# Gated layer of a two-part mix: all products stored first, then the down projection by 128-row blocks

## The chip, the core and the metric

The kernel runs on one core of a Trainium2 chip. The core has a matmul engine (TensorE, PE in the rows, with PEld for its weight loads), three engines for elementwise work (VectorE = DVE, ScalarE = ACT, GpSimd = POOL), and SyncE (SP), which here issues DMAs and passes on signals. The metric is the device time of one execution in microseconds; smaller is better.

## The reference

The input x has 2048 rows of 640 numbers, in four chunks of 512 rows. Two layers work on it and a gate per row mixes them:

```
x = A_x
g = _sigmoid((x * gate_w).sum(-1, keepdims=True))
a = _A_ref(x, A_wq, A_wk, A_wv, A_wo, A_beta)     # attention within a chunk, and a memory over chunks
b = _B_ref(x, B_w1, B_w3, B_w2)
return g * a + (1 - g) * b

def _B_ref(x, w1, w3, w2):                        # the gated layer
    gate = jnp.einsum("bsd,df->bsf", x, w1)
    up = jnp.einsum("bsd,df->bsf", x, w3)
    h = _silu(gate) * up                          # f = 1728
    return jnp.einsum("bsf,fd->bsd", h, w2)
```

Attention has 32 heads of 20 numbers. The change is about the gated layer alone.

## The kernel before

**Numbers.** Matmuls run in a reduced fp32 form (fp32r). For accuracy each operand is split into a high part (ScalarE casts it) and a low part (a subtraction on GpSimd or VectorE), and each product takes three passes (high by high, high by low, low by high; `PASSES`). `split` (line 172) does this to a weight.

**Halves of the array.** Nearly every product (a `Work`) is divided by its inner dimension: array rows 0 to 63 take one half of the 128, rows 64 to 127 the other, and both add to one PSUM bank. `halves` (line 254) makes the two lists. The two halves run at once on different works: while one work is in the second half, the next is in the first. Where a work moves from the first half to the second, an empty instruction on SyncE (`w.seen`, line 270) passes the signal. So SyncE's queue, which issues most DMAs, also stands in this path.

**Order.** The kernel writes every engine's order out itself. A planner keeps clocks of what each engine would do (`busy`, `clocks`, `heap`) and decides from them which instruction is written next; the program that results has a fixed order for each engine, with semaphores between them. A stream of dense works (projections and the gated layer) is pulled by `step`; attention comes in between by slots (`attention`, `S_AT`, `T_AT`): scores s with row maxima on VectorE, then transposed scores t, exponentials on ScalarE, a mask on GpSimd, and the weighted sums o. `segs` says which dense works lie beside which heads.

**Weights.** `w_add` puts a weight on a list. `w_load` brings item k into one of three raw buffers (`NRAW`); `w_split` splits it into one of eight tiles W (`NW`); `w_get` hands it to a matmul. Both are run in advance by `w_step`, or at once where a matmul needs the tile. `floors` and `set_oldest` say which tiles must still be kept. After a split the raw buffer counts as free only `FREE` = 2000 ns later.

**Gated layer.** w1 and w3 have 13 blocks of 128 columns and one (number 13, `NF`) of 64. For each pair of chunks, A = (0, 1) and B = (2, 3), and each block j, `ffn_up` makes g (gate) and u (up) for both chunks: ScalarE takes a tanh, VectorE multiplies twice, which leaves the product in a tile ft of 128 by 512. Then ScalarE copies it into ht (high) and GpSimd subtracts (low, line 1034). ht tiles are six (`NHT`). Because so few products fit, up and down alternate: five groups (`GROUPS`) of two or three blocks, and after each group `ffn_down` multiplies the ht tiles by the w2 blocks for every 128 rows (lb) and half of the 640 columns (hf), 8 tiles f per chunk. The first group's f is scaled and written to acc (ScalarE), the others are added to acc (VectorE, line 1103).

The attention's transfers qk<-qkd are issued by GpSimd (`load_pair`), between its splits. The attention's output projection is op (`oproj`); its adds to acc and those of f end the program, with the last stores.

Of the kernel before, what the change touches and what calls it, by code (L numbers as in the profile page):

```python
# [20 lines left out]
P = 128  # L21
# [9 lines left out]
NST, NW, NRAW, NHT, NVG, NB, FREE = 4, 8, 3, 6, 2, 8, 2000  # L31
# [9 lines left out]
R1H, R1B = 19, 3  # L41
COL, COL4, MIN_MM, APART, ISSUE, AHEAD = 0.4533, 1.7, 62, 5, 580, 1500
# [3 lines left out]
LAND, SPARE, NOP = 4200, 99999, 80  # L46
# [4 lines left out]
def gated_mix(ctx: ExitStack, tc: tile.TileContext, xT, wqk, wv, w13, w2, w2h, wo, beta, out):  # L51
# [9 lines left out]
    od = [dp.tile([H, 32, L], F32, name=f"od{c}") for c in range(NSEG)]  # L61
    gd = [dp.tile([P, 4, D], F32, name=f"gd{c}") for c in range(NSEG)]
# [109 lines left out]
    def split(dst, src, lo=None, ns=600, done=None, bank=None):  # L172

        def low():

            def sub(e):
                return lambda: e.tensor_sub(dst[:, 1], src, dst[:, 0].bitcast(F32))  # L177

            dve, pool = ("dve", 1.4 * ns, sub(nc.vector)), ("pool", 2.15 * ns, sub(nc.gpsimd))
            return dve if lo or busy["dve"] + dve[1] + SPARE < max(busy["pool"], now()) + pool[1] else pool  # L180

        stages(bank, ("act", ns, lambda: nc.scalar.copy(dst[:, 0], src)), low, done=done)  # L182
# [287 lines left out]
    def w_add(src, n, queue=nc.sync):  # L470
        items.append((src, n, queue))
        return len(items) - 1
# [6 lines left out]
    def limit():  # L479
        return NW + clock["oldest"] - sum(h < clock["oldest"] for s in floors.values() for h in s)  # L480
# [4 lines left out]
    def w_load():  # L485
        k = clock["next"]
        src, n, queue = items[k]
# [12 lines left out]
    def w_split():  # L500
        k, raw, n, _ = raws.pop(0)
        assert k < limit()
        w = sp.tile([P, 2, D + 2], FR, tag="W", name=f"W{k}", bufs=NW)
        halfway.add(k)

        def done():
            tiles[k] = w
            halfway.remove(k)
            if k not in EARLY:
                freed.append(now() + FREE)  # L510

        split(w[:, :, :n], raw[:, :n], k < NW, 730, done)

    halfway = set()

    def w_step():
# [8 lines left out]
        if clock["next"] < min(len(items), limit() + NRAW) and \  # L525
# [3 lines left out]
    def w_get(i):  # L529

        while i not in tiles:
# [5 lines left out]
            elif i in halfway:  # L537
                force()
# [88 lines left out]
    def new_x(c):  # L627
# [4 lines left out]
        while ("x", c - 2) in floors:  # L632
# [356 lines left out]
    def plan_down(js):  # L989
        return [w_add(w2[j] if j < NF else w2h, D) for j in js]  # L990

    hts = {}

    def ffn_up(cs, j, idx, oldest=None, by_weight=False, free=None, last=None):
        half = j == NF
        fs = {}

        def evac_gate(c):

            def evac(pg, bank):  # L1000
# [8 lines left out]
                a, b = (slice(0, 64), slice(64, P))[::-1 if c not in TURNED else 1]  # L1009
                u = f_tile(f"fu{c}_{j}")  # L1010
                ht = ht_tile([P, 2, L], FR, f"ht{c}_{j}")

                def end():
                    let(f"ft{c}_{j}")
                    let(f"fu{c}_{j}")
                    hts[c, j] = ht

                stages(bank, ("act", 600, lambda: nc.scalar.activation(t[:64], pg[:64], AF.Tanh, scale=0.5)),
                       ("dve", 690, lambda: nc.vector.scalar_tensor_tensor(u[64:], t[:64], 1.0, pg[:64], op0=ALU.add, op1=ALU.mult)),
                       ("dve", 690, lambda: nc.vector.scalar_tensor_tensor(pg[a], u[64:], 0.5, pg[64:], op0=ALU.mult, op1=ALU.mult)),  # L1020
                       ("act", 600, lambda: nc.scalar.copy(ht[a, 0], pg[a])),
                       ("dve", 690, lambda: nc.vector.tensor_sub(ht[b, 0], pg[a], ht[a, 0].bitcast(F32)), True), done=end)
            return evac

        def evac_up(c):

            def evac(pu, bank):
                ht = ht_tile([P, 2, L], FR, f"ht{c}_{j}")
# [3 lines left out]

                def low():
                    nc.gpsimd.tensor_sub(ht[:, 1], t, ht[:, 0].bitcast(F32))  # L1034

                def end():
                    let(f"ft{c}_{j}")
                    hts[c, j] = ht

                stages(bank, ("dve", 690, lambda: nc.vector.scalar_tensor_tensor(t, t, 0.5, pu, op0=ALU.mult, op1=ALU.mult), True),  # L1040
                       ("act", 620, lambda: nc.scalar.copy(ht[:, 0], t)), ("pool", 1290, low), done=end)  # L1041
# [3 lines left out]
        if by_weight:  # L1045
            todo.sort(key=lambda e: e[1])
        for n, (c, k) in enumerate(todo):
            old = min(idx[e[1]] for e in todo[n:]) if oldest is None else oldest
            name, evac = (("g", evac_gate(c)), ("u", evac_up(c)))[k]

            def end(ps, bank, evac=evac, n=n, c=c, k=k):
                evac(ps, bank)
                if last is not None:
                    last(c, j, idx[k])
                if free in floors and n == len(todo) - 1:
                    del floors[free]
# [5 lines left out]
    def ffn_down(cs, js, idx, last=False, free=None):  # L1062
        first = js[0] == 0
        def tile_of(c, lb, hf):

            def parts(ps):
                todo = [(j, i, a, b) for j, i in zip(js, idx) for a, b in (PASSES if j < NF else ((0, 0), (0, 1)))]
                return halves([lambda j=j, i=i, a=a, b=b: (ps[:, :320], hts[c, j][:, a, lb * P:(lb + 1) * P],
                                                           w_get(i)[:, b, 320 * hf:320 * hf + 320], 320 * COL)
                               for j, i, a, b in todo], 0, (c in TURNED, 3 * js.index(NF) + 1) if NF in js else None)  # L1070
# [12 lines left out]
            def evac(ps, bank):  # L1083
# [22 lines left out]
                if (lb, hf) == (3, 1):  # L1106
                    for j in js:
                        let(f"ht{c}_{j}")
                if free in floors and (c, lb, hf) == (cs[-1], 3, 1):
                    del floors[free]  # L1110

            return Work(f"f{c}_{js[0]}_{lb}_{hf}", parts, evac, idx[0], None, lambda: all((c, j) in hts for j in js) and (
                not first or c < NSEG - 1 or all(("out", 1, q) in landed for q in range(4))))

        for c in cs:
            if first:
                accs[c] = slot(f"acc{c}")[:, :4 * D].rearrange("p (b d) -> p b d", b=4)
            for lb in range(4):
                for hf in range(2):
                    yield tile_of(c, lb, hf)  # L1120
# [412 lines left out]
    GROUPS = [[0, 1, 2], [3, 4, 5], [6, 7, 8], [9, 10, 11], [13, 12], [9, 10], [13, 11, 12]]  # L1533

    def job_up(cs, j, by_weight=False):
        return (4 if j < NF else 2) * 3.5, ffn_up(cs, j, plan_up([j])[0], by_weight=by_weight)

    def woven(cs, j, c, first, mid):

        plan, key = plan_up([j])[0], ("w", cs, j)  # L1540
        floors[key] = set(plan)
        u = ffn_up(cs, j, plan, free=key)
        o1, o2 = jobs_oproj(c)

        def mix():
            yield from islice(o2[1], 4)
            yield from islice(u, mid)
            yield from o2[1]
            yield from u

        return o1, (3.5 * first, islice(u, first)), (3.5 * (4 - first) + o2[0], mix())

    def down_with_out(cs, g, c, mid):

        plan = plan_wo()
        floors["o", c] = held = set(plan)
        o1, o2 = oproj(c, plan, held)
        cost, f = job_down(cs, g)

        def mix():  # L1560
            yield from islice(o2, 4)
            yield from islice(f, mid)
            yield from o2
            yield from f

# [226 lines left out]
```

## Time and profile before

| | |
|---|---|
| three timed runs | 1077.18, 1077.37, 1078.13 us; median 1077.37 |
| profiled execution, first to last instruction | 1077.5 us |
| busy: TensorE, VectorE, ScalarE, GpSimd | 1070.5, 574.7, 491.0, 569.8 us |
| weight loads of TensorE (they overlap matmuls) | 975.3 us |
| moved by DMA | 154.98 MB, 144 GB/s on average |
| granted TensorE clock, mean | 0.998 |

No time for the profiled execution beyond its span is given; the span lies among the timed runs. In a group's row stand line, engine, operation, output<-inputs, shapes and count, then busy time (overlaps counted once), the mean length of one in ns, and the idle time of the engine before them, with what ended it. In the chain of waits a row has start, length, and the instruction. In a window's row stand the stretch, its length, busy time (and count) of PE, PEld, DVE, ACT and POOL, granted clock, DMA share and GB/s.

### The profile page before, as it was taken

The page shows a single profiled execution, that of the slowest core. Times are in us where ns is not written, and L with a number is a line of the kernel's source. Part 1 is how long each engine was busy: PE and PEld are TensorE (multiplying, and loading weights), DVE is VectorE, ACT ScalarE, POOL GpSimd, SP SyncE. Part 2 cuts the span into 40 slices and gives each one's busy share as a digit, 9 for nine tenths or more (in the row PEclk, how much of TensorE's full clock was granted, in tenths as well). Part 3 has the DMA queues.
Part 4 walks back from the last instruction along what each step waited for, and adds up shares of the span by engine and source line. Part 5 has one row for each costly group of instructions (what it writes and reads, how often), then busy time and mean ns, then how long its engine had stood idle before and what let it go on. Part 6 is the DMA issues. An engine that isn't in the chain of part 4 may idle for free.

```text
span 1077.5 us, 29709 instructions
## 1 busy us (share of the span) xinstructions
PE 1070.5 (99%) x11681; PEld 975.3 (91%) x11681; DVE 574.7 (53%) x1742; ACT 491.0 (46%) x1013; POOL 569.8 (53%) x765
## 2 busy tenths in 40 slices
PE   9999999999999999999999999999999999999998
PEld 7999999988998989889989989999889889888998
DVE  6022575345555666666454566663446666553464
ACT  6255434544344343465655664446442443344221
POOL 3543446366466464556664555655663854564340
PEclk9999999999999999999999999999999999999999
DMA  9465753243344331637585886554434542442231
GB/s 320 133 213 188 260 159 103 76 117 99 82 122 115 100 90 51 185 97 254 169 251 182 248 294 193 159 158 131 132 92 110 149 111 78 113 118 67 61 99 74
DMA packets 88099, 154.98 MB, mean 144 GB/s; under 512 B 19628, under 2 KB 34904, under 8 KB 87960
## 3 DMA queue, kind: packets, MB, share of 16 engines
q1 hardware_dynamic: 56520, 96.88, 27.7%
q0 software_dynamic: 23664, 42.04, 15.8%
q10 hardware_dynamic: 7776, 14.16, 3.7%
q8 instruction: 93, 1.52, 0.6%
q14 instruction: 46, 0.38, 0.1%
HBM read 97.55 MB, written 54.53 MB: 141 GB/s over the span
## 4 chain that ended last, share of the span: by engine, by line
PE 97%; DMA 1%; POOL 1%; issue 0%; ACT 0%; DVE 0%; POOLq 0%
PE g L267 19%; PE u L267 17%; PE f L267 16%; PE k L267 7%; PE o L1253 7%; PE v L267 7%; PE op L267 7%; PE q L267 5%; PE s L1158 4%; PE t L1220 4%; PE q L779 1%; PE pm L267 1%; PE nd L267 1%; DMA qk<-qkd 1%; PE pkt L265 0%; PE gt L265 0%
## 5 line engine op out<-in xcount | busy, mean ns | idle before, releaser
L267 PE MATMUL g<-X,W 64*128 64x512 f32 x1680 | 397.8, 395 | 0.0
L267 PE MATMUL u<-X,W 64*128 64x512 f32 x1560 | 378.8, 395 | 0.0
L1169 DVE CUSTOM_DVE_ANT_0 junk<-s,mask 128x128 bf16<-128x128 f32 (+3 forms) x512 | 251.2, 491 | 174.1 <-PE s L1158 135.7
L267 PEld LDWEIGHTS g<-X,W 64*128 64x128 f32 x1680 | 276.2, 185 | 13.4 <-issue 2.4
L177 POOL TENSOR_TENSOR W<-wr,W 128x640 fp32r<-128x640 f32 (+1 forms) x132 | 206.2, 1570 | 151.7 <-ACT W L182 139.0
L267 PE MATMUL f<-W,ht 64*128 64x320 f32 x2592 | 278.5, 309 | 0.0
L267 PEld LDWEIGHTS u<-X,W 64*128 64x128 f32 x1560 | 262.2, 185 | 9.6 <-issue 0.6
L267 PEld LDWEIGHTS f<-W,ht 64*128 64x128 f32 x2592 | 262.2, 187 | 2.2 <-issue 1.4
L1227 ACT ACTIVATE P<-t 128x384 f32<-128x384 f32 (+1 forms) x384 | 181.1, 525 | 148.8 <-PE t L1220 129.4
L1236 POOL TENSOR_SCALAR_AFFINE_SELECT P<-P 128x256 f32<-128x256 f32 (+1 forms) x192 | 93.5, 496 | 194.9 <-ACT P L1227 180.0
L182 ACT CAST W<-wr 128x640 fp32r<-128x640 f32 (+1 forms) x138 | 97.4, 726 | 43.6 <-PE u L267 24.9
L267 PE MATMUL k<-X,W 64*128 64x512 f32 x600 | 107.9, 399 | 0.0
L267 PE MATMUL op<-W,oT 64*128 64x320 f32 x960 | 103.5, 307 | 0.0
L267 PEld LDWEIGHTS op<-W,oT 64*128 64x128 f32 x960 | 97.8, 185 | 1.2 <-issue 0.8
L1103 DVE SCALAR_TENSOR_TENSOR acc<-f,cgate,acc 128x320 f32<-128x320 f32 x126 | 67.8, 547 | 55.8 <-PE f L267 52.7
L1158 PE MATMUL s<-qk 60*128 60x256 f32 (+2 forms) x512 | 90.1, 326 | 2.1 <-DMA qk<-qkd 2.1
L267 PE MATMUL v<-W,X 64*128 64x320 f32 (+2 forms) x948 | 90.7, 310 | 0.0
L1220 PE MATMUL t<-qk 62*128 62x256 f32 (+2 forms) x512 | 89.6, 324 | 0.0
L1034 POOL TENSOR_TENSOR ht<-ft,ht 128x512 fp32r<-128x512 f32 x52 | 67.2, 1293 | 41.0 <-ACT ht L1041 40.7
L1179 POOL DMA_DIRECT2D qk<-mr x128 | 73.4, 574 | 27.6 <-DVE mr L1195 25.5
L267 PEld LDWEIGHTS v<-W,X 64*128 64x128 f32 (+1 forms) x948 | 86.7, 186 | 0.6 <-issue 0.2
L267 PEld LDWEIGHTS k<-X,W 64*128 64x128 f32 x600 | 82.2, 185 | 3.6 <-issue 0.2
(121 smaller groups left out, 1307.2 us busy)
## 6 DMA issues: line engine op xcount, KB each, us to landing
qk<-qkd POOLq DMA_DIRECT2D x128, 240.0 KB, 4.0
wr<-in_w_dram SPq DMA_DIRECT2D x80, 320.0 KB
qkd<-qs SPq DMA_DIRECT2D x20, 512.0 KB
qkd<-ks SPq DMA_DIRECT2D x20, 512.0 KB
od<-oq ACTq DMA_DIRECT2D x32, 256.0 KB
wr<-in_wo_dram SPq DMA_DIRECT2D x20, 320.0 KB
vg<-vd SPq DMA_DIRECT2D x16, 336.0 KB
qkd<-qs SPq DMA_DIRECT2D x20, 256.0 KB
```

Of the source, the lines that this page charges most:

```text
L177: return lambda: e.tensor_sub(dst[:, 1], src, dst[:, 0].bitcast(F32))
L182: stages(bank, ("act", ns, lambda: nc.scalar.copy(dst[:, 0], src)), low, done=done)
L267: ins = nc.tensor.matmul(o, l, x, start=i == 0 and (r == 0 or not w.todo[0]), stop=i == len(todo) - 1 and (r == 1 or not w.todo[1]), skip_ ...
L1034: nc.gpsimd.tensor_sub(ht[:, 1], t, ht[:, 0].bitcast(F32))
L1103: nc.vector.scalar_tensor_tensor(dst, ps[:, :320], cgate[:, c, lb:lb + 1], dst, op0=ALU.mult, op1=ALU.add)
L1158: nc.tensor.matmul(ps[i][:, o:o + n], q[:, qb * P:(qb + 1) * P], k[:, :n], start=qb != 1, stop=qb != 0, skip_group_check=True)
L1169: nc.vector.tensor_tensor_reduce(out=junk[:, :n], in0=ps[i][:, o:o + n], in1=mask[:, L - n:], scale=1.0, scalar=-3.0e38, op0=ALU.add, op1= ...
L1179: nc.gpsimd.dma_start(dst, src)
L1220: nc.tensor.matmul(ps[i][:, o:o + L - q0], k[:, kb * P:(kb + 1) * P], q[:, q0:], start=kb != 2, stop=kb != 3, skip_group_check=True)
L1227: nc.scalar.activation(u["P"][:, i, o:o + n], ps[i][:, b:b + n], AF.Exp, scale=SCALE)
L1236: nc.gpsimd.affine_select(d, d, pattern=[[0, 2], [0, n], [1, P]], base=0, channel_multiplier=-1, compare_op=ALU.is_ge, fill=0.0)
L1253: nc.tensor.matmul(ps[32 * i:32 * i + 32, kb * P:], heads[2 * p + i]["v"][:, kb], pairs[p + i // 2]["P"][:, i % 2, o:o + n], start=kb == 0 ...
```

## The change

Up and down no longer alternate. `ffn_up` runs for all 14 blocks of a pair of chunks. Its product ft is not split; it is stored to a new DRAM tensor `hd` (60 stores by SyncE, from `send`), laid out by blocks of 128 rows. Then `ffn_down` runs in three groups of 4, 5 and 5 blocks of w2. For each group, chunk and block of 128 rows one item of the weights' list is the product itself: 128 by 512 or 640 numbers, loaded from `hd` like a weight (48 loads) and split like one. The two column halves of f use it in turn. VectorE takes a split of these items or of w2 when the planner finds it sooner there (`EVEN`). In groups 1 and 2, four of the five w2 blocks lie in what was a chunk's X tile (`home`, tile XW), since X is not needed once the products are made.

Buffers: W tiles 8 to 9, raw buffers 3 to 4, ht tiles 6 to 4. A raw buffer of such an item counts as free 700 ns after its split (`SOON`), not 2000. The helpers for mixed up and down work (`woven`, `down_with_out`, `jobs_up_by_chunk` and others) go, and the lists of segments are written anew: the output projections now follow f tiles of whole groups.

```diff
-NST, NW, NRAW, NHT, NVG, NB, FREE = 4, 8, 3, 6, 2, 8, 2000
+NST, NW, NRAW, NHT, NVG, NB, FREE = 4, 9, 4, 4, 2, 8, 2000
...
+    hd = [dp.tile([4, 3, P, D], F32, name=f"hd{c}") for c in range(NSEG)]
...
     def w_split():
         k, raw, n, _ = raws.pop(0)
         assert k < limit()
-        w = sp.tile([P, 2, D + 2], FR, tag="W", name=f"W{k}", bufs=NW)
+        home = items[k][5]
+        if home is None:
+            w = sp.tile([P, 2, D + 2], FR, tag="W", name=f"W{k}", bufs=NW)
+        else:
+            c, i = home
+            if i == 0:
+                homes[c] = cp.tile([P, 2, KB, L], FR, tag="X", name=f"XW{c}", bufs=2)
+            w = homes[c].rearrange("p a k l -> p (a k l)").rearrange("p (i a n) -> p i a n", i=4, a=2)[:, i]
...
-                freed.append(now() + FREE)
+                freed.append(now() + (FREE if items[k][4] is False else SOON))
...
-        split(w[:, :, :n], raw[:, :n], k < NW, 730, done)
+        split(w[:, :, :n], raw[:, :n], k < 8, 730 * n / D, done, spare=EVEN if items[k][4] else SPARE)
...
+        def send(c, t):
+            name = f"ft{c}_{j}"
+            todo = [(slice(0, 64), t[64:]), (slice(64, P), t[64:])] if half else [(slice(0, P), t)]
...
+            for k, src in list(todo):
+                dst = hd[c][:, g, k, n * P:(n + 1) * P].rearrange("b p n -> p b n")
+                store_later(dst, src.rearrange("p (b n) -> p b n", n=P), ("h", c, j, k.start), done=end)
...
-                def low():
-                    nc.gpsimd.tensor_sub(ht[:, 1], t, ht[:, 0].bitcast(F32))
...
                 stages(bank, ("dve", 690, lambda: nc.vector.scalar_tensor_tensor(t, t, 0.5, pu, op0=ALU.mult, op1=ALU.mult), True),
-                       ("act", 620, lambda: nc.scalar.copy(ht[:, 0], t)), ("pool", 1290, low), done=end)
+                       done=lambda: send(c, t))
...
-    GROUPS = [[0, 1, 2], [3, 4, 5], [6, 7, 8], [9, 10, 11], [13, 12], [9, 10], [13, 11, 12]]
+    GROUPS = [[0, 1, 2, 3], [4, 5, 6, 7, 8], [9, 10, 11, 12, 13]]
...
+    def job_down(cs, g, at=range(8), last=False):
+        js = GROUPS[g]
+        wi, after = plans.setdefault((cs, g), []), plans.setdefault((cs, g + 1), [])
+        wi += [plan_down(cs, g, n) for n in range(len(wi), len(js))]
+        n = len(js) * P
+        hi = {}
+        for a in at:
+            c, lb = cs[a // 4], a % 4
+            hi[c, lb] = w_add(hd[c][lb, g, :, :n], n, even=True,
+                              needs=[("h", c, j, k) for j in js for k in ((0, 64) if j == NF else (0,))])
+            if a in NEXT[g]:
+                after.append(plan_down(cs, g + 1, len(after)))
...
-    tail = [braid(chain([d] + u + [d2, take(d3, 6)]), o1, 1400, 6000), alternate(take(o2, 7), take(d3, 0)), o2, d3]
+    d2 = job_down(B, 2, last=True)
+    o1, o2 = jobs_oproj(3)
+    tail = [braid(chain([d1b, take(d2, 14)]), o1, 1400, 6000), o2, d2]
```

What this does to the written order is shown at two places. The first is ScalarE where chunk 3 follows chunk 2 in the first down group of pair B. Before (acc_11654 is chunk 2's, acc_12115 chunk 3's; P are exponentials of t):

```order
L1087 ACTIVATE acc_11654<-f_0_1_1_11946,cgate 128x320
L1087 ACTIVATE acc_11654<-f_0_2_0_11973,cgate 128x320
L1087 ACTIVATE acc_11654<-f_0_2_1_12030,cgate 128x320
L1087 ACTIVATE acc_11654<-f_0_3_0_12053,cgate 128x320
L1227 ACTIVATE P_12058<-t_1_0_12166 128x384
L1227 ACTIVATE P_12058<-t_1_1_12167 128x384
L1087 ACTIVATE acc_11654<-f_0_3_1_12083,cgate 128x320
L182 CAST W_12202<-wr_12076 128x640
L1087 ACTIVATE acc_12115<-f_0_0_0_12117,cgate 128x320
L182 CAST W_12228<-wr_12109 128x640
```

ScalarE now, at the same place (acc_14629 is chunk 2's; W_14946 and W_14996 are the first two product blocks of chunk 3; oq is the copy of a group of weighted sums, od its store):

```order
L1110 ACTIVATE acc_14629<-f_0_1_0_14711,cgate 128x320
L184 CAST XW_14650<-wr_14761 128x640
L1110 ACTIVATE acc_14629<-f_0_1_1_14754,cgate 128x320
L1280 COPY oq_14936<-o_14919 128x512
L716 DMA od_79<-oq_14936 128x512
L184 CAST W_14946<-wr_14788 128x512
L1110 ACTIVATE acc_14629<-f_0_2_0_14790,cgate 128x320
L1249 ACTIVATE P_14956<-t_0_0_14957 128x512
L1249 ACTIVATE P_14956<-t_0_1_14958 128x512
L184 CAST XW_14650<-wr_14801 128x640
L1110 ACTIVATE acc_14629<-f_0_2_1_14826,cgate 128x320
L184 CAST W_14996<-wr_14845 128x512
```

The casts of product blocks and of the next group's w2 stand between the evacuations, and the cast of chunk 3's first block comes after the copy and the store of o.

VectorE takes the low parts of both blocks; its rows there now (L1191 are row maxima over scores s, two instructions each):

```order
L179 TENSOR_TENSOR XW_14650<-wr_14761,XW_14650 128x640
L179 TENSOR_TENSOR W_14946<-wr_14788,W_14946 128x512
L1191 ISA junk,m_14729<-s_1_0_14992,mask 128x384
L1191 ISA m_14729 128x1
L1191 ISA junk,m_14729<-s_1_1_14993,mask 128x384
L1191 ISA m_14729 128x1
L1191 ISA junk,m_14729<-s_2_0_15015,mask 128x512
L1191 ISA m_14729 128x1
L1191 ISA junk,m_14729<-s_2_1_15016,mask 128x512
L1191 ISA m_14729 128x1
L179 TENSOR_TENSOR W_14996<-wr_14845,W_14996 128x512
```

The second block's subtraction stands behind four row maxima.

The second place is the end of TensorE's queue. Before, its last rows are all in the second half of the array (op is the output projection of chunk 3, f its last down tiles):

```order
L267 MATMUL op_3_1_17407<-W_16714,oT_17107 128x320
L267 MATMUL op_3_1_17407<-W_16723,oT_17107 128x320 x3
L267 MATMUL op_3_1_17407<-W_16845,oT_17107 128x320 x3
L267 MATMUL op_3_1_17407<-W_16976,oT_17107 128x320 x3
L267 MATMUL f_13_3_0_17441<-W_16259,ht_13_16798 128x320
L267 MATMUL f_13_3_0_17441<-W_16322,ht_12_17022 128x320 x3
L267 MATMUL f_13_3_1_17454<-W_16259,ht_13_16798 128x320
L267 MATMUL f_13_3_1_17454<-W_16322,ht_12_17022 128x320 x3
```

TensorE's last rows now (the three rows without a count alternate: f_2_3_1 in the first half of the array, f_2_3_0 in the second; the last four rows are all in the second half):

```order
L269 MATMUL f_2_3_1_17356<-XW_15853,W_16701 128x320
L269 MATMUL f_2_3_0_17327<-XW_15853,W_16701 128x320
L269 MATMUL f_2_3_1_17356<-W_16361,W_16701 128x320
L269 MATMUL f_2_3_0_17327<-XW_15853,W_16701 128x320 x8
L269 MATMUL f_2_3_0_17327<-W_16361,W_16701 128x320 x2
L269 MATMUL f_2_3_1_17356<-XW_15853,W_16701 128x320 x12
L269 MATMUL f_2_3_1_17356<-W_16361,W_16701 128x320 x2
```

The run in one half alone has 8 + 2 + 12 + 2 = 24 matmuls where it had 18 (those rows of before, from the first to the last); it now consists of f tiles of five blocks instead of op and f tiles of two.

214 lines of the change are left out of this document (95 added, 119 removed).

## The prediction

> **What bounds the kernel now.** I read the share of busy time first, then the costliest groups, then the chain that ended last and the windows around its few breaks.
>
> ```profile
> span 1077.5 us, 29709 instructions
> PE 1070.5 (99%) x11681; PEld 975.3 (91%) x11681; DVE 574.7 (53%) x1742; ACT 491.0 (46%) x1013; POOL 569.8 (53%) x765
> ...
> L267 PE MATMUL g<-X,W 64*128 64x512 f32 x1680 | 397.8, 395 | 0.0
> L267 PE MATMUL u<-X,W 64*128 64x512 f32 x1560 | 378.8, 395 | 0.0
> L267 PE MATMUL f<-W,ht 64*128 64x320 f32 x2592 | 278.5, 309 | 0.0
> L267 PE MATMUL k<-X,W 64*128 64x512 f32 x600 | 107.9, 399 | 0.0
> L267 PE MATMUL op<-W,oT 64*128 64x320 f32 x960 | 103.5, 307 | 0.0
> L1158 PE MATMUL s<-qk 60*128 60x256 f32 (+2 forms) x512 | 90.1, 326 | 2.1 <-DMA qk<-qkd 2.1
> L267 PE MATMUL v<-W,X 64*128 64x320 f32 (+2 forms) x948 | 90.7, 310 | 0.0
> L1220 PE MATMUL t<-qk 62*128 62x256 f32 (+2 forms) x512 | 89.6, 324 | 0.0
> ...
> L267 PE MATMUL q<-X,W 64*128 64x512 f32 x480 | 83.0, 395 | 0.0
> L779 PE MATMUL q<-X,W 128*128 128x512 f32 x59 | 14.6, 402 | 0.0
> ```
>
> TensorE is busy for all but 7.0 us. A mean of 395 ns says little about its pace, since matmuls overlap; the chain of waits gives the pace, because it goes from one TensorE instruction to the next (start, length, what):
>
> ```profile
> 738.58 1.62 PE f L267 x22
> ...
> 917.52 2.38 issue
> 922.09 3.11 POOL W L177 x2
> 925.67 6.70 DMA qk<-qkd
> ...
> 952.88 5.47 DMA qk<-qkd
> ...
> 1005.62 2.29 PE o L1253 x32
> ...
> 1022.25 4.21 PE g L267 x36
> ...
> 1072.71 1.19 PE f L267 x8
> ```
>
> A 320-column half-array matmul advances the chain by 1.62/22 = 0.074 us when both halves of the array work, a 512-column one by 4.21/36 = 0.117, a group of weighted sums (o) by 2.29; the last eight f, in one half alone, take 0.149 each. With the counts above: g, u, k and 480 q are 4320 x 0.117 = 505 us; 59 q on the whole array, twice that each, 14; f, op and v are 4500 x 0.074 = 333; 1024 s and t at a mean width of 352 columns (0.080) 82; 32 groups o 73; the 754 that are left of the 11681 (1024 records are o's) are narrower than 320 columns, so under 0.074 each, and I take 35. That is about 1042 of 1077.5 us. Start and end take some 8 (the windows below, and a first q near 5 us). About 28 us, 2.6%, is all that a better order of the same matmuls can still win, over the whole program. **TensorE's order and its waits decide**; the other engines count only where they make it wait.
>
> The three timed runs lie from 1077.18 to 1078.13 us with a median of 1077.37; the profiled span agrees, so I sum against 1077.5 and subtract 0.1.
>
> **Where TensorE loses time now.** Windows (length, busy time and count by engine, granted clock, DMA share, GB/s) and the DMA issues before one loss:
>
> ```profile
> 900.00:950.00 50.00, 48.52 (x591) 44.85 (x590) 28.88 (x97) 18.82 (x40) 24.07 (x33) 0.97 0.38 101
> 950.00:1000.00 50.00, 49.38 (x481) 42.93 (x479) 18.95 (x57) 24.50 (x51) 28.78 (x37) 1.00 0.32 90
> 1050.00:1078.00 28.00, 23.88 (x301) 23.62 (x297) 12.12 (x24) 4.13 (x9) 2.03 (x2) 0.97 0.19 72
> ...
> 930.00:933.00 3.00, 1.52 (x18) 1.12 (x15) 0.60 (x2) 0.97 (x2) 2.91 (x7) 0.99 1.12 313
> 933.00:937.00 4.00, 4.00 (x38) 3.81 (x39) 2.41 (x10) 0.72 (x1) 3.98 (x4) 0.58 0.34 57
> ...
> 923.66 0.57 SPq L1138 DMA_DIRECT2D vg<-vd  x1
> 925.13 1.10 POOL L1134 DMA_DIRECT2D qk<-qkd  x2
> 925.24 3.15 SPq L495 DMA_DIRECT2D wr<-in_w_dram  x3
> ```
>
> At 930 us TensorE stood for 1.5 us, because the score matmuls (s, whose row has the idle time) waited for a qk transfer that was issued among a vg load and three weight loads at 313 GB/s. After it the granted clock was 0.58 over 4 us, a loss of another 4.00 x 0.42 = 1.7 us. The window from 950 lacks 0.6 more, with a late qk in the chain again. These 3.8 us are the losses that can be seen singly in the second half.
>
> **The change part by part.**
>
> *What stays.* TensorE gets the same matmuls: 1680 g, 1560 u, 2592 f, each of the same width. No term of the 1042 us changes.
>
> *Evacuations of f.* Each pair of chunks had five down groups and gets three, so 32 x 2 = 64 evacuations of f fewer; all are additions to acc on VectorE, or the few on ScalarE.
>
> ```profile
> L1103 DVE SCALAR_TENSOR_TENSOR acc<-f,cgate,acc 128x320 f32<-128x320 f32 x126 | 67.8, 547 | 55.8 <-PE f L267 52.7 <-PE v L267 2.5
> L177 POOL TENSOR_TENSOR W<-wr,W 128x640 fp32r<-128x640 f32 (+1 forms) x132 | 206.2, 1570 | 151.7 <-ACT W L182 139.0
> L1034 POOL TENSOR_TENSOR ht<-ft,ht 128x512 fp32r<-128x512 f32 x52 | 67.2, 1293 | 41.0 <-ACT ht L1041 40.7
> ...
> 1045.78 4.07 DVE L1103 SCALAR_TENSOR_TENSOR acc<-f,cgate,acc 128x320 f32<-128x320 f32 x7
> ```
>
> 62 x 0.547 = 34 us leave VectorE. There they mostly lay beside TensorE work. Where f tiles were short (two and a half columns of weights, 1045 us) seven evacuations ran back to back for 4.07 us, so banks came free late. With four or five columns of weights a tile lasts 12 to 15 x 0.149 = 1.8 to 2.2 us in its half, and an evacuation of 0.547 fits. The row of f shows no idle time before it, so the worth lies between 0 and the whole 28 us; nearest is 0, and I take **-1.0**.
>
> *Splits of the products.* 52 splits of ht leave ScalarE and GpSimd; 48 of h come. Of h and w2 together, 41 that were not there are VectorE's now, and GpSimd has 7 more W splits than before: 52 x 1.293 - 7 x 1.570 = 56 us less on GpSimd.
>
> ```profile
> L177 DVE TENSOR_TENSOR W<-wr,W 128x640 fp32r<-128x640 f32 x1 | 0.8, 820 | 0.0
> ```
>
> On VectorE 41 x 0.820 = 34 us take the place of the 34 that left, so it gets no freer. GpSimd's transfer issues for qk stand in its queue behind splits (above: 3.11 us of W, then the late qk), so fewer splits there make that stall less likely. I count both visible stalls as gone: **-3.8**, bounded by 0 and -3.8. Whether they stay away rests on the next term.
>
> *Traffic.* Products go to DRAM and back: 52 x 256 KB and 8 half ones out, 48 loads of 256 or 320 KB in, some 29 MB on 155.
>
> ```profile
> qk<-qkd POOLq DMA_DIRECT2D x128, 240.0 KB, 4.0
> wr<-in_wqk_dram POOLq DMA_DIRECT2D x10, 320.0 KB, 5.3
> ```
>
> The mean, 144 GB/s, becomes about 171, well under the 313 seen. But the down stages now take a 320 KB load for every 60 f, 4.4 us of TensorE: 73 GB/s on top of the 90 to 100 there, and a qk transfer that meets a crowd lands in 6.7 us, not in 4.0. The price of one such meeting is the 3.2 us above. I take a fifth of one, **+0.6**, between 0 and three (9.6). SyncE issues 108 transfers more; its queue also holds the handoffs that let the second half of the array start, and a store that waits for its product holds them up. The products are written a whole tile ahead of most handoffs, so nothing is added, with the bound of one short wait each in a tenth of the cases, 60 x 0.1 x 0.4 = 2.4.
>
> *Just-in-time splits.* In the first down group of chunks 2 and 3 ScalarE's and VectorE's order shows a copy of o, an od issue, the cast and VectorE's subtraction in a row, all after one o group, before the first f of chunk 3, with 30 f and 2 t between.
>
> ```profile
> L1041 ACT CAST ht<-ft 128x512 fp32r<-128x512 f32 x52 | 32.3, 622 | 51.3 <-DVE ft L1040 51.2
> L1258 ACT COPY oq<-o x32: 586/587/588, 171.9 to 1008.0; 128x512 f32<-128x512 f32 x32
> L689 ACTq DMA_DIRECT2D od<-oq x32: 326/326/354, 172.6 to 1008.6; - x32
> ...
> L177 DVE TENSOR_TENSOR oT<-oall,oT x32: 414/548/1025, 395.3 to 1064.7; 128x256 fp32r<-128x256 f32 x16, 128x384 fp32r<-128x384 f32 x16
> ```
>
> That is 0.587 + 0.326 + 0.622 + about 0.69 (an estimate for 512 columns, from 820 for 640 and a median of 548) = 2.2 us against 30 x 0.074 + 2 x 0.117 = 2.5 us. A quarter of a microsecond is the cover; the next block, behind four row maxima, has as little. Likely waits of 0.3 us at two blocks: **+0.6**. If a wait there reaches the 1.5 us of 930, the clock adds 1.7.
>
> The last row bears on it: a subtraction of two SBUF tiles took up to 1025 ns where 548 is usual. [...]
>
> *End.* Before, 18 matmuls of one half stand behind the last of the other half; now 24, since the last f tile has 14 in that half and the tile before it 10 more (the order at the end of TensorE's queue, above): 6 x 0.149 = **+0.9**.
>
> **Sum:** -1.0 - 3.8 + 0.6 + 0.6 + 0.9 = -2.7 us; 1077.5 - 2.7 - 0.1 = 1074.7.
>
> **Rivals.** (1) *More is won.* Banks and handoffs are the hidden loss, and long f tiles win a third of the 28 us, or 9: 1077.4 - 9 + 1 = about 1069. For it: f is 192 of the 1042 us, and up and down alternate five times per pair now. Against it: no idle time in the rows of f, g and u. (2) *Nothing is won.* The qk wait is a meeting of transfers and returns elsewhere: 1077.4 - 1.0 + 0.6 + 0.9 = 1078. For it: lead times of those loads in the new order are no longer than before. [...] That the change doesn't do what it says is no rival: the order shows the groups, stores and tiles.
>
> **How the numbers follow.** Forecast 0.45, centre 1074.7, 1072 to 1077.5 by itself; rival 1 0.18; rival 2 0.15; rival 3 0.22. A run of this kernel can tell about 0.2%, 2.2 us, from no change: faster is below 1075.2, slower above 1079.5. Of the forecast some 0.28 is below 1075.2; rival 1 wholly, so faster 0.46. Same: 0.17 of the forecast and 0.12 of rival 2, 0.29. Slower: 0.03 and rival 3, 0.25. The range runs from a little under rival 1, 1066, to 1085, two meetings of transfers above rival 2.
>
> **What would show it.** Right: no PE wait for qk over 1 us after 900 us, no granted clock below 1 before the end, f evacuations of 0.55 us with idle before each, and a longer one-half end of about 3.5 us. Wrong: PE or its weight loads waiting for W, idle at the head of chunks 1 and 3 with a clock of 0.5 after it, or SyncE's DMA issues held by ft. More than 8 us either way would mean that the hidden part of the 28 us, not the visible stalls, is what the change moves.

## The result: 1.1% slower, and the profile after

| | before | changed |
|---|---|---|
| timed runs | 1077.2 to 1078.1, median 1077.65 us (4) | 1087.5 to 1092.2, median 1089.86 us (4) |
| ratio | | 1.0111, 95% interval 1.0093 to 1.0129 |
| profiled span | 1077.5 us | 1087.1 us |
| moved by DMA | 154.98 MB, 144 GB/s | 184.36 MB, 170 GB/s |

The changed kernel is 12.2 us slower. The page of its profile:

```profile
span 1087.1 us, 29863 instructions
...
PE 1073.8 (99%) x11681; PEld 966.5 (89%) x11681; DVE 581.7 (54%) x1717; ACT 483.5 (44%) x1003; POOL 513.3 (47%) x718
...
L269 PE MATMUL f<-XW,W 64*128 64x320 f32 x1536 | 160.9, 310 | 3.6 <-SPq L272 3.6
```

And from its groups by line, the additions of f to acc on VectorE:

```profile
L1126 DVE SCALAR_TENSOR_TENSOR acc<-f,cgate,acc 128x320 f32<-128x320 f32 x64 | 35.0, 549 | 51.6 <-PE f L269 51.2
```

TensorE has the same 11681 instructions, GpSimd 56 us less work, as worked out. PE's busy time rose by 3.3 us and its idle time by 6.3, with f's mean length as before (310 and 309 ns): the waits are short, and a busy PE hides part of them (51.4 us lost by the count below, where PE is idle for 13.3). TensorE's own waits in the changed kernel (total us, times, longest):

```profile
PE f L269 <- SPq L272: 3.6, 2, 2.2
PE s L1180 <- DMA qk<-qkd: 1.8, 3, 1.0
PE t L1242 <- DMA qk<-mr: 1.4, 2, 1.0
...
PE t L1242 <- DVE gm L844: 0.9, 1, 0.9
```

Before, s waiting for qk was alone here but for the first matmuls of all, with 2.1 us (the idle time in its row). Now there are four kinds, none over 4 us in all, and 0.8 us of t that end in no wait the profile shows. TensorE's waits for the transfers of attention (s for qk, t for the row mr in it) did not shrink: 3.2 us now, 2.1 before. The windows that answer to those shown of before, and two in which the new losses lie:

```profile
400.00:450.00 50.00, 47.76 (x632) 44.28 (x631) 28.25 (x83) 24.29 (x49) 28.70 (x37) 0.99 0.62 169
450.00:500.00 50.00, 50.00 (x653) 48.47 (x653) 32.48 (x91) 23.18 (x46) 24.73 (x29) 0.97 0.49 144
...
900.00:950.00 50.00, 48.43 (x534) 41.65 (x531) 28.90 (x93) 25.32 (x54) 21.54 (x33) 1.00 0.49 136
950.00:1000.00 50.00, 50.00 (x668) 46.77 (x667) 27.17 (x80) 29.06 (x61) 25.51 (x34) 1.00 0.51 144
1000.00:1050.00 50.00, 48.68 (x674) 46.81 (x672) 26.89 (x49) 15.79 (x27) 17.72 (x18) 1.00 0.58 181
```

The clock's fall moved: 0.97 stood from 900 us before, and stands from 450 us now. To see also what busy time hides, I took from the trace, for each half of the array, the time from the start of a matmul to the start of the next, less its columns times 0.453 ns (232 ns for 512 columns, the usual step from one g or u to the next in a half; narrow kinds at their usual length, the o groups left out). What is left is lost time, a falling clock included. In us by stretch, mean of both halves (two arbitrary other orders of the kernel before are explained further down):

| stretch, us | before | changed | before, split age 4500 | before, column time 0.460 |
|---|---|---|---|---|
| 0 to 350 | 10.0 | 11.5 | 11.5 | 13.1 |
| 350 to 550 | 4.7 | 11.0 | 7.1 | 8.0 |
| 550 to 750 | 8.6 | 12.7 | 11.3 | 14.9 |
| 750 to 1000 | 11.0 | 7.5 | 7.7 | 9.0 |
| from 1000 | 7.8 | 8.7 | 7.7 | 7.7 |
| all | 42.1 | 51.4 | 45.3 | 52.7 |

Between 750 and 1000 us 3.5 us less are lost, close to the forecast gain in size. But TensorE's idle time there is as before (2.1 us, now 2.0), and 1.7 of the 3.5 us are the clock's fall, which now stands in the second row. Against them stand 6.3 us more in pair A's down stage and what follows it, and 4.1 us between 550 and 750, where no f of the changed kernel runs at all.

### The profile page after: what moved, and what is told of

It is laid out like the page before. It is cut to its first block, busy times and chain, and to the rows that moved or that the text cites. A ratio compares the mean times of both kernels' runs of the same rounds, so it can differ in the third digit from the quotient of the medians.

```text
span 1087.1 us, 29863 instructions
## 1 busy us (share of the span) xinstructions
PE 1073.8 (99%) x11681; PEld 966.5 (89%) x11681; DVE 581.7 (54%) x1717; ACT 483.5 (44%) x1003; POOL 513.3 (47%) x718
## 2 busy tenths in 40 slices
DMA packets 124645, 184.36 MB, mean 170 GB/s; under 512 B 21356, under 2 KB 65304, under 8 KB 124504
## 4 chain that ended last, share of the span: by engine, by line
PE 92%; DMA 3%; POOL 1%; issue 1%; DVE 1%; ACT 1%; SPq 0%; POOLq 0%; DVEq 0%
PE g L269 17%; PE f L269 17%; PE u L269 15%; PE k L269 7%; PE v L269 7%; PE op L269 6%; PE o L1275 6%; PE q L269 5%; PE s L1180 4%; PE t L1242 4%; PE q L806 1%; PE pm L269 1%; DMA qk<-qkd 1%; PE nd L269 1%; DMA qk<-mr 1%
## 5 line engine op out<-in xcount | busy, mean ns | idle before, releaser
L269 PE MATMUL g<-X,W 64*128 64x512 f32 x1680 | 377.1, 394 | 0.0
L269 PE MATMUL u<-X,W 64*128 64x512 f32 x1560 | 351.9, 394 | 0.0
L1191 DVE CUSTOM_DVE_ANT_0 junk<-s,mask 128x128 bf16<-128x128 f32 (+3 forms) x512 | 251.2, 491 | 161.7 <-PE s L1180 122.1
L179 POOL TENSOR_TENSOR W<-wr,W 128x640 fp32r<-128x640 f32 (+2 forms) x133 | 206.5, 1557 | 177.2 <-ACT W L184 165.7
L269 PEld LDWEIGHTS u<-X,W 64*128 64x128 f32 x1560 | 244.4, 185 | 14.4 <-issue 1.2
L269 PE MATMUL f<-XW,W 64*128 64x320 f32 x1536 | 160.9, 310 | 3.6 <-SPq L272 3.6
L269 PEld LDWEIGHTS f<-XW,W 64*128 64x128 f32 x1536 | 153.8, 186 | 4.6 <-SPq L272 4.1
L184 ACT CAST W<-wr 128x640 fp32r<-128x640 f32 (+2 forms) x170 | 119.7, 719 | 54.8 <-PE u L269 19.3
L269 PE MATMUL f<-W,W 64*128 64x320 f32 x1056 | 138.6, 309 | 0.0
L269 PEld LDWEIGHTS f<-W,W 64*128 64x128 f32 x1056 | 118.8, 186 | 1.2 <-issue 1.0
L269 PE MATMUL v<-W,X 64*128 64x322 f32 (+2 forms) x948 | 89.2, 310 | 0.0
```

Of the source, the lines that this page charges most:

```text
L269: ins = nc.tensor.matmul(o, l, x, start=i == 0 and (r == 0 or not w.todo[0]), stop=i == len(todo) - 1 and (r == 1 or not w.todo[1]), skip_ ...
L1191: nc.vector.tensor_tensor_reduce(out=junk[:, :n], in0=ps[i][:, o:o + n], in1=mask[:, L - n:], scale=1.0, scalar=-3.0e38, op0=ALU.add, op1= ...
```

## The experiments

The expectations of the first four kernels (late x loads and the three on stores) spell their theories out. From then on theory S says that the product blocks' loads and splits cost the time; theory C, that single places lost the work that covered them; theory O, formed after eight kernels, that any order other than the one of before costs as much. Each ratio is to the kernel before on the same chip, whose median lay from 1077.6 to 1078.3 us in all batches; the changed kernel itself was not run again beside them.

**A hold in SyncE's queue.** The largest single loss lies at 447 us. SyncE's waits from 440 to 455 us, its DMA issues, TensorE's next matmuls after its stand (the wait in brackets), and two windows of the changed kernel:

```profile
SPq L716 <- PE op L269: 5.5, 1, 5.5
```

```profile
447.31 2.23 SPq L716 DMA_DIRECT2D xr<-in_xT_dram  x5
```

```profile
449.65 2.50 PE L269 MATMUL f<-XW,W 64*128 64x320 f32 x15 [2.24 <-SPq L272]
```

```profile
446.00:449.00 3.00, 1.41 (x18) 1.10 (x15) 1.38 (x2) 2.42 (x6) 1.01 (x2) 1.00 0.33 82
449.00:453.00 4.00, 3.35 (x26) 3.35 (x28) 0.61 (x3) 0.57 (x1) 2.46 (x2) 0.57 0.86 304
```

Five loads of x for chunk 2 write into the tile that holds oT of chunk 0. They wait 5.5 us for the last projection matmuls, and the handoff of the next f tile is queued behind them. When the wait is over, SyncE still takes 2.23 us to issue the five, and for just that long, 2.24 us, TensorE stands (1.6 us of it in the first window). Then it runs at 0.57 of the clock. The first experiment puts two f tiles ahead of the loads (`xs` is the later work on x):

```diff
-o2, (0, load_raw(2)), braid(chain([d1b, d2]), xs, ...)
+o2, braid(chain([(0, islice(d1b[1], 2)), (0, load_raw(2)), d1b, d2]), xs, ...)
```

> The changed kernel, with the five loads of chunk 2's x two f tiles later, behind the handoff of the first f of chunk 1's second group. Handoff theory (these loads wait in SyncE's queue for the output projection to release their buffer, and hold up the signal behind them; TensorE lost 2.5 us and then 1.7 us at half clock there): about 4 us less, 1086 for 1090. Traffic theory (29 MB more on the DMA queues make attention's transfers land later): no change, 1090. Split theory (just-in-time splits at the heads of chunks): no change.

1087.26 us (1084.5 to 1088.2), 1.0080 [1.0068, 1.0092], 2.6 us less than the changed kernel. The edit leaves ScalarE's and VectorE's instructions in the order that they had. The windows have recovered:

```profile
400.00:450.00 50.00, 50.00 (x668) 46.77 (x667) 29.08 (x86) 24.68 (x50) 28.67 (x37) 1.00 0.61 163
450.00:500.00 50.00, 49.90 (x666) 48.06 (x665) 33.43 (x96) 25.84 (x51) 28.15 (x32) 1.00 0.57 167
```

A second hold of this kind ends at 1015.7 us: the load of chunk 3's sums has waited 4.1 us for the landing of the last od store. In the kernel with late x loads:

```diff
-            after(6, o_sums, c)
+            after(6 if c < NSEG - 1 else 12, o_sums, c)
```

> Changed kernel with the x loads late, and the load of the last chunk's sums issued six steps of 700 ns later, so that SyncE no longer stands 4.1 us for the landing of the last od store with handoffs behind it. Theory C (handoffs behind a waiting DMA issue): the stall of 1.4 to 1.6 us at 1014 us goes: 1085.5 to 1086.2. If the later sums only move the wait to the normalization of chunk 3: 1087 or a little above.

1086.28 us, 1.0079 [1.0066, 1.0093]: 1.0 us less, as theory C has it, though the two intervals overlap.

**The stores.** Three kernels ask what the 60 stores cost: without them (the blocks' loads then read w2, so the gated layer's result is another), 52 such stores (the half blocks left out) added to the kernel before and never read, and the stores issued by ScalarE.

```diff
-store_later(dst, src..., ("h", c, j, k.start), done=end)
+stored.add(...); landed.add(...); end()
```

> The changed kernel without the 60 stores of products; the product blocks are loaded from blocks of w2 of the same size, so the gated layer's result is another one. Traffic theory: half of the added bytes and 29 thousand packets of 512 bytes go, so the waits for qk transfers and for row maxima go back to the few of before, 4 to 6 us less, 1084 to 1086. Handoff theory: only what stores hold in SyncE's queue goes (63 us of waits for products), 0 to 2 us less; the 4 us at chunk 1's second group stay. Split theory: no change.

> The kernel before, with 52 stores of the same products (256 KB each, 512-byte pieces, from SyncE) added and never read. Traffic theory: 2 to 5 us more than before, 1080 to 1083. Handoff theory: 0 to 2 us more, by holds in SyncE's queue. Split theory: no change, 1077.7.

```diff
-store_later(dst, src..., done=end)
+store_later(dst, src..., nc.scalar, done=end)
```

> The changed kernel with the 60 stores issued by ScalarE. Traffic theory: no change, 1090, or up to 1 us more for 60 issues of 0.33 us on ScalarE. If it is the stores' waits in SyncE's queue that hold handoffs: 2 to 4 us less, 1086 to 1088. Split theory: no change.

1088.93 us (1086.4 to 1091.7), no gain that stands out from the changed kernel's 1089.86; 1078.88 against 1078.29, 1.0010 [1.0001, 1.0018]; and 1098.48, 1.0172 [1.0145, 1.0200]. So the stores cost about 0.6 us in the kernel before, an amount that would not stand out in the changed one, and SyncE is the better place. The longest waits of the kernel with ScalarE's stores show why: an exponential stood 5.8 us behind two stores, and the next t of TensorE 3.8 us for it. A part of its loss is the clock: its six runs go from 1091.5 us with a mean clock of 1.000 to 1102.5 us with 0.993.

```profile
PE t L1242 <- ACT P L1249: 3.8, 1, 3.8
...
ACT P L1249 <- DMA hd<-ft: 5.8, 1, 5.8
```

**The product blocks.** Neither loaded nor split; the left sides come from the w2 tile that is there.

```diff
-            hi[c, lb] = w_add(hd[c][lb, g, :, :n], n, even=True, ...)
+            hi[c, lb] = len(items)
-    w_get(hi[c, lb])[k, a, n * P:(n + 1) * P]
+    w_get(wi[n])[k, a, lb * P:(lb + 1) * P]
```

> Changed kernel with the five x loads of chunk 2 late (1087.3 us before this), and in it the 48 product blocks are neither loaded nor split: the left sides of the down matmuls come from the w2 tile that is there already, so the gated layer's result is another. TensorE's matmuls, the stores of the products and the w2 splits stay. If the loads and just-in-time splits of the blocks are what was mis-sized (theory S), the two waits at the heads of chunks 1 and 3 (1.8 and 0.8 us), what the clock adds, and the crowded qk landings go: 1080 to 1083. If the loss sits in places where the new order has no cover, whatever the blocks do (theory C: o-projection tiles back to back, handoffs through SyncE), it stays at 1085 to 1088.

1087.23 us (1085.4 to 1089.4), the same as 1087.26 with them. The page shows the work gone:

```profile
span 1083.7 us, 29618 instructions
...
PE 1073.9 (99%) x11681; PEld 966.9 (89%) x11681; DVE 560.7 (52%) x1689; ACT 453.9 (42%) x955; POOL 483.8 (45%) x698
```

Against the kernel with late x loads ScalarE has 30 us less, GpSimd 31, VectorE 20, and the time doesn't move. TensorE's waits for qk and mr did shrink, from 4.0 us to 1.8 in the profiled executions, without a gain in the median. So theory S has nothing for it here, though with four and five runs that spread over 4 us a cost of a microsecond or so would not be seen, and beside the down groups other instructions change places with the blocks gone. It also had a milder test, the next group's w2 beside later blocks:

```diff
-    plans, NEXT = {}, (range(1, 5), range(4, 8), ())
+    plans, NEXT = {}, (range(4, 8), range(4, 8), ())
```

> Changed kernel with the x loads late, and the next group's four w2 tiles loaded beside blocks 4 to 7 of the first down group in place of blocks 1 to 4, so that the first blocks have ScalarE's casts, the landing buffers and the DMA queue for themselves up to the head of the second chunk. Theory S: the wait of 1.8 us at the head of chunk 1 and that of 0.8 us at chunk 3 shrink by half or go: 1084.5 to 1086. If they only move to the next block: 1087, no change from 1087.3. Theory C says no change too.

1087.88 us, 1.0105 [1.0086, 1.0124]. The 1.8 us at the head of chunk 1 went in its trace, and 3.8 us came at 957 us (each in one half of the array), before the first f of the second group, which starts at 960.46 us behind a signal of ScalarE: the lost time moved.

**The projection's cover.** Before, `down_with_out` broke the eight projection tiles op of chunks 0, 1 and 2 with f tiles after the fourth; now they run in a row. One kernel breaks them again (shown for chunk 2, two or four other tiles after the fourth op), one takes the break from the kernel before.

```diff
-seg = [braid(chain(u + [d0, d1]), o1, 2400, 1500), o2]
+seg = [braid(chain(u + [d0, d1]), o1, 2400, 1500), mix(o2, islice(d1b, 4))]
```

> Changed kernel with the x loads late, and the eight output-projection tiles of chunks 0, 1 and 2 broken in the middle by other tiles as in the kernel before: after four of them two f tiles of the next blocks (chunk 0), the four tiles of one up job (chunk 1), four f tiles (chunk 2). Theory C: back-to-back projection tiles had left SyncE's handoffs and the casts of oT for the third and fourth row block without cover; 1082 to 1085, and the handoff waits at op1 and behind them (1.0, 1.0, 1.0 us between 705 and 740) shrink. Theory S: the split waits stay and so does the time, 1086.5 to 1088.

```diff
         def mix():
-            yield from islice(o2, 4)
-            yield from islice(f, mid)
             yield from o2
             yield from f
```

> Kernel before, with the output-projection tiles of chunks 0, 1 and 2 no longer broken by f tiles: eight in a row and then the f tiles, as in the changed kernel. Theory C: SyncE's handoffs and the casts of oT lose their cover here too, +1.5 to +3 us: 1079 to 1081. If the weave mattered only through what the changed kernel has around it: 1077.5 to 1078.5.

1084.78 us (1083.9 to 1087.0), 2.5 less than without; and 1079.81 against 1077.89, 1.0019 [1.0011, 1.0028], 1.9 more. Both directions agree, so the lost break is worth about 2 us. The second is the cleaner test: of ScalarE's 870 instructions other than weight splits it moves 15 to another place in the order, the first one 257 of 812, and an order written anew can by itself be worth more than 2 us (below). And the places do not add up:

> Changed kernel with the x loads of chunk 2 late, the output projections of chunks 0, 1 and 2 broken by other tiles (two f tiles, one up job, two f tiles), and the next group's w2 beside blocks 4 to 7 in the first pair of chunks alone. Theory C (many places without cover, each worth 1 to 3 us, that add up): 1081 to 1083.5, since the weaves alone came to 1084.8 with a wait of 3.0 us at 697 us and 2.8 at the end, and the wait at the head of chunk 1 is 1.5. A theory by which the time follows the amount of work and traffic of the two stages and the places only move: 1084 to 1086.

1086.14 us (1084.3 to 1089.2): with three repairs together it is no better than with the breaks alone. By the count of lost time in one half, the handoff of the first k waits 2.6 us at 534, where 1.0 stood with the breaks alone, and the waits at 696 (3.0, now 2.7) and at the head of op3 (2.8, now 1.8) are still there. A sum of repaired places misses here too.

**Other orders.** That led to theory O. Two figures of the planner were varied in both kernels, in the changed one with the x loads late: how long after its load a weight may be split (`AGE`, 5000 ns), and the estimate of a matmul's time per column (`COL`, 0.4533 ns). Neither is an operation; they only shift what is written next. But they are not quite without meaning, as the expectations have it: one is the planner's estimate of TensorE's pace, the other the time that it leaves between a load and its split, so a trial also plans by another picture of the chip.

```diff
-NP, AGE = 2, 5000
+NP, AGE = 2, 4500
```

> Kernel before, with one figure of the planner's that has no meaning on the chip changed (a weight tile may be split 4500 ns after its load in place of 5000), so that the same work comes in a slightly other order everywhere. If the time before rests on its waits having been ordered away place by place (theory O), an arbitrary other order costs 2 to 6 us: 1080 to 1084. If the staging makes the difference and the order is worth little, 1077 to 1079.

> Changed kernel with the x loads late, and the same planner figure changed as in the kernel before (4500 ns in place of 5000). Theory O: an order that nobody has worked over moves either way by a microsecond or two, 1085.5 to 1089 against 1087.3, while the kernel before only gets worse. If the staging sets the time: 1087 within half a microsecond.

> Kernel before with the planner's figure at 4000 ns. Theory O (the time before rests on an order in which the waits are hidden): 1080 to 1084, as 4500 gave 1082.7. If 4500 was one unlucky place: 1077.5 to 1079.

> Kernel before with the planner's figure at 5500 ns. Theory O: 1080 to 1084. If only an earlier split costs something, since it takes ScalarE and a buffer too soon: 1077.5 to 1079.

> Changed kernel with the x loads late, the planner's figure at 4000 ns. If all of the 12 us is order, the changed kernel's orders scatter like the other's, around 1081 to 1084, and some come near 1080. If the stages cost something by themselves, they stay 3 to 5 us above the mean of the kernel before's arbitrary orders: 1085 to 1088.

> Changed kernel with the x loads late, the planner's figure at 5500 ns. As for 4000 ns: 1081 to 1084 if all is order, 1085 to 1088 if the stages cost 3 to 5 us by themselves.

> Kernel before with the planner's estimate of a matmul's time per column at 0.460 ns in place of 0.4533, which moves places of the order everywhere from the first chunk on. Theory O (the time before rests on its one order): 1081 to 1090. If only the age of a landed weight matters, since splits too early or late have a cost of their own: 1077.5 to 1079.5.

> Changed kernel with the x loads late and the same figure at 0.460. By its order 4 of SyncE's handoffs stand less than 0.7 us of TensorE work behind what they wait for, where 14 do with 0.4533. If handoffs without lead are what the orders differ in: 1081 to 1084. If the loss sits in many kinds of waits that no single lead tells: 1085 to 1090, as for the other orders.

| median, us | as written | 4500 | 4000 | 5500 | column 0.460 |
|---|---|---|---|---|---|
| kernel before | 1077.9 | 1082.65 | 1089.79 | 1086.14 | 1092.30 |
| changed, x loads late | 1087.26 | 1086.33 | 1087.86 | 1091.39 | 1098.23 |

Against its own runs on the same chip (1077.9 to 1078.2) the kernel before loses 4.8, 11.8, 8.1 and 14.1 us by orders that nobody meant to be worse, 9.7 on average; one such order alone (1092.3) is slower than the changed kernel. Theory O had the direction; three of the four lie above the range that it gave. The changed kernel moves either way (-0.9, +0.6, +4.1, +11.0), and its last two lie above every forecast. The mean of its four other orders lies 3.2 us above that of the kernel before; the four differences are 3.7, -1.9, 5.3 and 5.9, so their mean is uncertain by about 1.8 and a cost of the two stages themselves is possible, not shown. With the column time of 0.460 both kernels lose much, 14.1 and 11.0 us, so this figure may do more than reshuffle; with the three ages the kernel before loses 8.2 us on average and the changed one 1.3, as theory O would have it. What a figure off its value costs by itself, and what the other order costs, was not tried apart. My count of SyncE handoffs without lead failed as an indicator: 4 against 14, and the slowest time of all.

One place shows how such an order loses. At the head of chunk 1's projection, 700 to 720 us, the kernel before, then with 4000 ns, then with a column time of 0.460:

```profile
700.00:720.00 20.00, 20.00 (x259) 18.34 (x259) 14.77 (x50) 9.90 (x22) 12.20 (x18) 1.00 0.51 140
```

```profile
700.00:720.00 20.00, 18.70 (x141) 15.65 (x141) 12.32 (x38) 7.76 (x18) 14.13 (x17) 0.83 0.46 119
```

```profile
700.00:720.00 20.00, 18.40 (x148) 14.49 (x148) 12.20 (x39) 8.07 (x18) 12.79 (x17) 0.83 0.52 143
```

Over 110 matmuls fewer begin in these 20 us. The clock of 0.83 alone is 20 x 0.17 = 3.4 us in each; the fall came with a stand of TensorE (1.3 and 1.6 us). Waits of the last one from 700 to 715 us, and after them VectorE's timeline there (start, length):

```profile
ACT oT L182 <- DVE oall L1360: 3.7, 1, 3.7
...
PEld op L267 <- DVE oT L177: 1.9, 1, 1.9
PE op L267 <- DVE oT L177: 1.6, 1, 1.6
```

```profile
711.82 0.69 DVE L1040 SCALAR_TENSOR_TENSOR ft<-ft,u 128x512 f32<-128x512 f32 x1
712.42 0.68 DVE L1360 TENSOR_TENSOR oall<-oall,gt 128x512 f32<-128x512 f32 x1
713.02 2.02 DVE L177 TENSOR_TENSOR oT<-oall,oT 128x256 fp32r<-128x256 f32 x4
```

The last addition to oall came behind a product ft and three gm on VectorE; ScalarE's casts of oT waited 3.7 us for it, the subtractions followed, and op stood. In the kernel before that addition began at 698.48 us and op at 700.6, with the casts between:

```profile
698.48 0.69 DVE L1360 TENSOR_TENSOR oall<-oall,gt 128x512 f32<-128x512 f32 x1 [2.25 <-PE gt L265]
```

In the changed kernel the same op begins at 712.1 us behind a cast of oT. No f tile and no product block is near it; what differs is which up tiles and which attention stand beside it. That the 12 us of the changed kernel are losses of this kind all over is an inference from these places and trials: the hold at 447 us and the break were shown one by one (2.6 and 1.9 us), the hold at 1015 us within the noise (1.0), the rest not.

## Why the prediction was wrong, by its steps

- **The sum itself failed**, in the sentence that about 28 us "is all that a better order of the same matmuls can still win". I used those 28 us as room for gains and never asked what an unplanned order would lose. TensorE's matmuls stayed, so I took the places of everything else between them as unchanged in worth, and added up only what the diff names: a term put at nothing. TensorE's order is another from the first k tiles on. The runs show in its place 2.6 us for the x loads, 1.0 (within the noise) for the sums and 1.9 for the projection's break, and that other orders of the kernel before cost it 4.8 to 14.1 us. How the rest of the miss divides between the order and the two stages stays open. The last sentence of the prediction said what a miss of this size would mean: the hidden part of the 28 us.
- **qk stalls, -3.8.** This step failed too, though 3.5 us less are lost between 750 and 1000 us. The reason given, fewer splits in front of GpSimd's transfer issues, did not take the waits away: s and t of the changed kernel wait 3.2 us for attention's transfers against 2.1, at 247, 799, 937 and 944 us among others, and before the last matmul the clock fell once, as before, only at 449 us (0.57 over 4 us, 0.58 before). Rival 2 had this, that the qk wait returns elsewhere. That the size between 750 and 1000 us is near the forecast one is luck.
- **Base.** "The profiled span agrees, so I sum against 1077.5 and subtract 0.1" was wrong. In all timed runs of the experiments the time is 1.7 to 2.0 us above the span, and the kernel before has a median span of 1076.3 us (59 runs). The profiled execution was a slow one by about 1.2 us. The clock's 1.7 us in it was mostly not there to win: the profile's mean clock was 0.998, and 57 of the 59 timed runs have 0.999 or 1.000.
- **Traffic, +0.6.** Near in size: the stores alone added 0.6 us to the kernel before, and qk lands in 4.5 us at the median, not 4.0. A fifth of one meeting was a guess, and what the loads of the blocks cost was not measured apart.
- **SyncE, "nothing is added".** Right for the stores, which wait 62.7 us in all in SyncE's queue without being missed; wrong for the queue: x loads and sums that had had cover now hold handoffs up, 2.6 and 1.0 us. The prediction priced the DMAs that the change adds, not those that it moves.
- **The projection's break** was in the diff (`down_with_out` goes) and in no term: about 2 us.
- **Just-in-time splits, +0.6.** Lost time came where it was placed, 1.8 us in one half of the array at chunk 1 and 0.8 at chunk 3, where a t also stood 1.0 us for its transfer. It did not set the time, since without the blocks the time is the same (1087.23 us, 1087.26 with them). That waits for splits set it, to which rival 3 gives its 0.22, no run shows; what the runs showed in its place are the 2.6, 1.9 and 1.0 us named first.
- **End, +0.9.** In size right: the chain's last f row is 4.16 us for 33 matmuls, 24 in one half at 0.149 and nine at the two-half pace (0.074) are 4.2.

```profile
1079.59 4.16 PE f L269 x33
```

- **Evacuations, -1.0.** 64 additions on VectorE in place of 126, at 549 ns where it was 547. What that is worth was not tried apart.

No kernel tried here beats the one before; the best of the changed ones is 1084.78 us. Whether the two stages, with an order worked over as long as the other's, would end below 1077 stays open.

## What to carry to other kernels

Where one engine is 99% busy and a planner writes the order, vary a figure of the planner a little before pricing a change: the scatter of the unchanged kernel's time (here 5 to 14 us, all upward, in four trials) is a first estimate of what an edit that writes the order anew can cost, and it belongs into the forecast as a term. Price the DMAs and tiles that an edit moves past a queue as carefully as those it adds. Compare the profiled execution with the timed runs by span and clock before a stall in it is counted as something to win.

## What the runs showed of the hardware

After a stand of 2.24 us at 447 us the granted clock was 0.57 over 4 us, and 0.58 after two of 0.35 and 1.13 us at 930 us before. The length of a stand does not decide alone: the kernel without stores stood 2.24 us at 447.9 us, for the same five loads, and its clock stayed at 1.00 (the same window as above):

```profile
449.00:453.00 4.00, 2.87 (x38) 2.88 (x40) 1.22 (x5) 1.05 (x2) 2.95 (x2) 1.00 0.89 314
```

The subtraction of a 512-column product block, which I had estimated at 0.69 us, took 0.69 with GpSimd idle and 1.20 with two masks on GpSimd beside it (VectorE's timeline, start and length):

```profile
378.35 1.20 DVE L179 TENSOR_TENSOR W<-wr,W 128x512 fp32r<-128x512 f32 x1 [0.93 <-ACT W L184]
...
943.52 0.69 DVE L179 TENSOR_TENSOR W<-wr,W 128x512 fp32r<-128x512 f32 x1 [3.60 <-issue]
```

Subtractions of 640 columns show it more clearly. One at 376.60 us took 0.82 us, with only DMA issues on GpSimd beside it; the one below took 2.01, with a subtraction on GpSimd beside it (VectorE first, then GpSimd):

```profile
428.39 2.01 DVE L179 TENSOR_TENSOR XW<-wr,XW 128x640 fp32r<-128x640 f32 x1
...
428.16 1.56 POOL L179 TENSOR_TENSOR W<-wr,W 128x640 fp32r<-128x640 f32 x1 [0.62 <-ACT W L184]
```

GpSimd had begun 0.23 us before, and VectorE took the 1.33 us that were left of it and 0.68 us more. The kernel's time did not visibly depend on it: 1087.23 us without the blocks' subtractions, 1087.26 with them.
